# Cached attention and MLP, two passes on one core: paired K transfers, a split last V, an earlier output preparation, a norm in two powers, half blocks on two queues, and another pace for row 0

## The chip, the cores and the metric

The kernel runs on one core of one Trainium2 chip. Its time is the device time in microseconds (us). For the kernel before, five runs gave 1109.03 to 1117.27 us, with a median of 1114.41 us. One further execution was recorded by the hardware profiler. All stage times below come from that execution, counted from the start of its span.

## What is computed

Eight rows of 448 values (B = 8, one token each) go through four residual blocks: attention over a cached K and V, an MLP block, and the same two again with the same weights and the same caches.

```python
def _A_ref(x, k_cache, v_cache, wq, wo):      # 16 query heads, 8 K/V heads, 4096 positions, 256 per head
    q = (x @ wq).reshape(B, Sq, Hq, Dh).transpose(0, 2, 1, 3)
    k = jnp.repeat(k_cache, rep, axis=1); v = jnp.repeat(v_cache, rep, axis=1)
    p = _softmax(jnp.einsum("bhqd,bhkd->bhqk", q, k) * (Dh ** -0.5), axis=-1)
    o = jnp.einsum("bhqk,bhkd->bhqd", p, v)
    return o.transpose(0, 2, 1, 3).reshape(B, Sq, Hq * Dh) @ wo
...
x = A_x
x = x + _A_ref(_layernorm(x, axis=-1), A_k_cache, A_v_cache, A_wq, A_wo)
x = x + _B_ref(_layernorm(x, axis=-1), B_w1, B_w2, B_w3, B_w4)
x = x + _A_ref(_layernorm(x, axis=-1), A_k_cache, A_v_cache, A_wq, A_wo)
x = x + _B_ref(_layernorm(x, axis=-1), B_w1, B_w2, B_w3, B_w4)
```

With one token per row the shifts inside `_B_ref` leave nothing of its first half, so the kernel computes only `x + gelu(layernorm(x) @ w3) @ w4` there, with two layernorms in a row folded into one helper (`norm` with `twice`).

The K cache and the V cache hold 134 MB each in bf16. A row's second pass needs the result of its first pass, so a row's K and V are wanted twice.

## The kernel before

The caches are cut into tiles of 1 MB: 128 partitions of 8 KB. A pair of K/V heads (`gp`, four of them) of one row has four K tiles and four V tiles. A K tile takes, for each partition, one contiguous run of 8 KB out of that partition's 32 KB of the cache, so that two neighbouring K tiles (c = 0 and 1, or 2 and 3) are neighbours in memory as well. Tiles lie in 15 "places", slices of one SBUF tile (`places_t`, `slots`).

The work is a list of 512 items (`items`, L532 to L541), one for each use of a tile, in which the K tiles of one head pair alternate with the V tiles of the pair before. `ps` is the pass (0 or 1), `b` the row, `n` the task, `c` the tile's number. Eleven K and V tiles of each row (`kept`, L63) stay in their places between the first and the second pass, and a twelfth (`inner`) waits in PSUM. That leaves 416 loads instead of 512. While the eleven tiles of a row stay, four places are left for everything that streams by. When the second pass has used them, their places come free within a few items.

`emit_loads` (L603) is called after each item. It takes the loads in order, asks `place_for` (L575) for a free place, and issues one DMA of 1 MB on SP's queue at L624. A load that finds no place ends the call, and those behind it wait as well. For K tiles of the heads that stay, `place_for` looks for two adjacent places and reserves the second (`held`). If two such tiles do lie side by side, `scores` multiplies both in one instruction of 256 columns instead of two of 128 (`also`, L817).

For a K item the VectorE makes two 32x32 block transposes (L632, `transpose_k`) and TensorE the scores (L647). After every second K tile ScalarE makes the exponentials (L656). For a V item TensorE accumulates the product of the probabilities with V (L702). In the last row's last two head pairs the outputs come as columns (`pv_cols`, L716), followed at once by their share of the output projection (`add_cols`, L337). SP's loads wait on semaphores for the place's last reader, and each also waits for the transfer eight before it, since eight DMA semaphores are used in turn.

The small work of a row (the output projection's halves, norms, MLP, next query) is cut into steps of Python generators (`first_half`, `chain`, `first_last`, `last`, `rest`), and `step` (L754) slips one step of each kind in twice per item. `add_gen` takes the items between which a generator is to be spread. Only one generator of a kind runs at a time: the `chain` of row 0 starts when its `first_half` is through.

`load_split` (L160) brings a weight of 448 input rows: three blocks of 128 rows, then the last 64 rows in two halves of columns, one to partitions 0 to 63 (L163) and one to partitions 64 to 127 (L164).

`norm` (L196) forms 1/sqrt as a power on GpSimd (L241). With `twice` it forms two values for each row in one instruction: value 1 scales what goes into the next matmul (`xb`, L261), value 0 updates the residual (L272). For one row or four rows in the MLP this is 2 or 8 values.

After the loop (L885 on) the residual is updated, an fp32 identity (`ident2`) and a zeroed PSUM tile (`o_row`) are made, the last four rows' MLP is run, and the four quarters of the output are written.

Of the kernel before, what the change touches and what calls it, by code (L numbers as in the profile page):

```python
# [8 lines left out]
FP32 = mybir.dt.float32  # L9
# [3 lines left out]
ALU = mybir.AluOpType  # L13
EPS = 1e-5
# [3 lines left out]
def kernel(  # L18
# [27 lines left out]
    nc = tc.nc  # L46
# [14 lines left out]
    NC = 15  # L61
# [98 lines left out]
    def load_split(t, src, cols):  # L160
        for fc in range(3):
            nc.sync.dma_start(t[:, fc * cols : (fc + 1) * cols], src[fc * 128 : fc * 128 + 128, :])
        nc.sync.dma_start(t[0:64, 3 * cols :], src[384:448, 0 : cols // 2])  # L163
        nc.sync.dma_start(t[64:128, 3 * cols :], src[384:448, cols // 2 :])  # L164

    wq_sb = split_tile(HD, "wq_sb")
    w3_sb = split_tile(F, "w3_sb")
# [28 lines left out]
    def norm(x, nb, twice):  # L196

        def room(name, shape, at):  # L200
            n = shape[0] * shape[1]
            if nb < Bn:
                t = chn.tile([128, n * MID], FP32, tag=name)
                ap = t[:, 0 : n * nb]
            else:
                ap = scratch(at, n * nb)
            return ap.rearrange("p (s f b) -> p s f b", s=shape[0], f=shape[1])

        def bc(ap):
            return ap.unsqueeze(1).to_broadcast([128, 4, nb])  # L210

        xx = room("xx", (2, 4), 0)
        nc.vector.tensor_mul(xx[:, 0], x, wv[:].unsqueeze(2).to_broadcast([128, 4, nb]))
        nc.vector.tensor_mul(xx[:, 1], xx[:, 0], x)
        xs = room("xs", (1, 2), 512)[:, 0]
        nc.vector.tensor_reduce(
            xs, xx.rearrange("p s f b -> p s b f"), mybir.AxisListType.X, ALU.add
        )
        yield
        st = room_ps("st", nb).rearrange("p (s b) -> p s b", b=nb)  # L220
        nc.tensor.matmul(st, ones, xs, start=True, stop=True)
        yield
        mv = room("mv", (1, 2), 528)[:, 0]
        nc.vector.tensor_copy(mv, st)
        var = room("var", (1, 1), 608)[:, 0, 0]
        if nb == 1:
            nc.vector.scalar_tensor_tensor(
                var, mv[:, 0], mv[:, 0], mv[:, 1], ALU.mult, ALU.subtract, reverse1=True
            )
        else:  # L230
            nc.vector.tensor_mul(var, mv[:, 0], mv[:, 0])
            nc.vector.tensor_sub(var, mv[:, 1], var)


        ve = room("ve", (1, 2), 544)[:, 0]
        n = 2 if twice else 1
        nc.vector.tensor_scalar(ve[:, 0], var, 0.0, EPS, ALU.max, ALU.add)
        if twice:
            nc.vector.tensor_scalar(ve[:, 1], var, 0.0, EPS * EPS / (1 + EPS), ALU.max, ALU.add)
        rs = room("rs", (1, 2), 560)[:, 0]  # L240
        nc.gpsimd.tensor_tensor(  # L241
            rs[:, 0:n].rearrange("p n b -> p (n b)"),
            ve[:, 0:n].rearrange("p n b -> p (n b)"),
            nhalf[:].to_broadcast([128, n * nb]),
            ALU.pow,
        )
        xc = room("xc", (1, 4), 576)[:, 0]
        nc.vector.tensor_tensor(xc, x, bc(mv[:, 0]), ALU.subtract)  # L248
        yield
        if nb > 1:  # L250
            yield
        c = (1 + EPS) ** -0.5 if twice else 1.0
        rl = rs[:, n - 1]
        parts = ((0, 128, 0, 0, 3, 0), (0, 64, 64, 3, 4, 3), (64, 128, 64, 3, 4, 4))
        for p0, p1, x0, f0, f1, to in parts:
            pp = slice(x0, x0 + p1 - p0)
            dst = xbs(nb)[p0:p1, to : to + f1 - f0, :]
            if nb == 1:
                nc.vector.tensor_scalar(dst, xc[pp, f0:f1], rl[pp], c, ALU.mult, ALU.mult)
            else:  # L260
                nc.vector.scalar_tensor_tensor(  # L261
                    dst,
                    xc[pp, f0:f1],
                    c,
                    rl[pp].unsqueeze(1).to_broadcast([p1 - p0, f1 - f0, nb]),
                    ALU.mult,
                    ALU.mult,
                )
        if twice and nb == 1:
            nc.vector.scalar_tensor_tensor(x, xc, rs[:, 0], x, ALU.mult, ALU.add)  # L270
        elif twice:
            nc.vector.tensor_tensor(xc, xc, bc(rs[:, 0]), ALU.mult)  # L272
            nc.vector.tensor_add(x, x, xc)
        yield
# [175 lines left out]
    def first_half(b, st):  # L450

        OT = work.tile([128, 2, Hq, 1], BF16, tag="OT", bufs=1)
        st["OT"] = OT
        yield from half(st["o", 0], st["z"], 0, OT[:, :, :, 0])
        yield from add_cols(
            y_room(1)[:, 0], lambda i: OT[:, i % 2, i // 2], wo_sb, range(NB2 // 2), 1
        )
# [85 lines left out]
    def stays(it):  # L543
        n, kv, c = it
        return (tasks[n][2], kv, c) in kept
# [10 lines left out]

    held = {}
    AHEAD = 4

    def paired(n, c):  # L560

        ps, _, gp = tasks[n]
        u = c - c % 2
        if ps == 0:
            return gp in keep
        return all((gp, 0, k) in kept for k in (u, u + 1))
# [8 lines left out]
    def place_for(it):  # L575

        n, kv, c = it
        if it in held:
            p = held.pop(it)
            if p not in places:  # L580
                held[it] = p
                return None
            places.remove(p)
        else:
            open_ = [p for p in places if p not in held.values()]
            if not open_:
                return None
            p = open_[0]
            if kv == 0 and c % 2 == 0 and paired(n, c):
                two = [  # L590
                    (max(free_at[q], now[0]), k, p1, q)
                    for k, p1 in enumerate(open_)
                    for q in (p1 + 1, p1 - 1)
                    if 0 <= q < NC and q not in held.values() and free_at[q] <= now[0] + AHEAD
                ]
                if two:
                    _, _, p, q = min(two)
                    held[n, 0, c + 1] = q
            places.remove(p)
        free_at[p] = again[tasks[n][1:], kv, c] if tasks[n][0] == 0 and stays(it) else used_at[it]  # L600
        return p

    def emit_loads(most=None):  # L603
        n = 0
        while loads and places and n != most:
            it = loads[0]
            p = place_for(it)
            if p is None:
                break
            del loads[0]  # L610
            where[it] = p
            if stays(it):
                where[tasks[it[0]][1:], it[1:]] = p
            t, kv, c = it
            _, b, gp = tasks[t]
            dst = slots[p]
            rows = (A_v_cache if kv else A_k_cache)[b, 2 * gp : 2 * gp + 2].rearrange(
                "g s d -> (g s) d"
            )
            if kv:  # L620
                src = rows.rearrange("(a p y) d -> a p (y d)", a=4, y=16)[c]
            else:
                src = rows.rearrange("(p x y) d -> x p (y d)", x=4, y=16)[c]
            nc.sync.dma_start(dst[:], src)  # L624
            n += 1

    def transpose_k(t):
# [123 lines left out]
    def add_gen(kind, b, g, at, until, total):  # L751
        gens.append({"kind": kind, "b": b, "g": g, "at": at, "until": until, "n": 0, "of": total})
# [20 lines left out]
    rz_gp = None  # L773

    for idx, it in enumerate(items):
        n, kv, c = it
        ps, b, gp = tasks[n]
        if (ps, b, gp, kv, c) == (0, Bn - 1, REST, 0, 0):
# [50 lines left out]
        else:  # L829
# [34 lines left out]
            if c == 3:  # L864
                done = pairs_done[ps, b] = pairs_done.get((ps, b), 0) + 1
                if done == 2 and ps == 0:
                    add_gen("chain", b, first_half(b, st), idx + 1, idx + 21, 10)
                elif done == 2:
                    add_gen("chain" if final else "last", b, first_last(b, st), idx + 1, idx + 13, 9)
                elif done == 4 and ps == 0:  # L870
                    add_gen("chain", b, chain(b, st), idx + 1, first_of[(1, b), 0] - 1, 38)
                elif done == 4 and not final:
                    add_gen("last", b, last(b, st), idx + 1, idx + (7 if b == Bn - 2 else 13), 6)
# [8 lines left out]
        step(10 * len(items))  # L882


    end = [slots[p] for p in places[:2]]  # L885
    xs = xT[:, :, MID:]
    nc.vector.tensor_add(xs, xs, st["y"])
    ident2 = end[0][:, 0:256].bitcast(FP32)
    nc.vector.tensor_copy(ident2, identb[:])
    W = D // 4  # L890
    o_row = store[0][:, 0:W]
    nc.vector.memset(o_row, 0.0)
    run(mlp_hidden(MID, Bn - MID))
    for q in range(4):
        for fc in range(4):
# [57 lines left out]
```

The softmax here doesn't subtract the row's maximum and nothing guards it: scores larger than these inputs give would overflow.

## Time and profile before

| what | us |
|---|---|
| median of five runs | 1114.41 |
| the profiled execution: its time | 1115.8 |
| the profiled execution: its span | 1114.0 |
| TensorE busy in matmuls / in weight loads | 663.6 / 461.3 |
| VectorE busy | 592.9 |
| ScalarE busy | 124.3 |
| GpSimd busy | 15.7 |
| VectorE idle until a K tile landed | 278.3 |
| TensorE idle until a V tile landed | 89.4 |
| last matmuls on the last V tile start | 1099.93 |

Busy time is the sum of the instructions of an engine[...]. 448.96 MB pass over the DMA engines in the span, a mean of 403 GB/s. The granted TensorE clock was full until about 190 us and then mostly half, 0.636 in the mean.

### The profile page before, as it was taken

The page shows a single profiled execution, that of the slowest core. Times are in us where ns is not written, and L with a number is a line of the kernel's source. Part 1 is how long each engine was busy: PE and PEld are TensorE (multiplying, and loading weights), DVE is VectorE, ACT ScalarE, POOL GpSimd, SP SyncE. Part 2 cuts the span into 40 slices and gives each one's busy share as a digit, 9 for nine tenths or more (in the row PEclk, how much of TensorE's full clock was granted, in tenths as well). Part 3 has the DMA queues.
Part 4 walks back from the last instruction along what each step waited for, and adds up shares of the span by engine and source line. Part 5 has one row for each costly group of instructions (what it writes and reads, how often), then busy time and mean ns, then how long its engine had stood idle before and what let it go on. Part 6 is the DMA issues. An engine that isn't in the chain of part 4 may idle for free. (4 is left out here: it accounts for less than half of the span.)

```text
span 1114.0 us, 33816 instructions
## 1 busy us (share of the span) xinstructions
PE 663.6 (60%) x15606; PEld 461.3 (41%) x15606; DVE 592.9 (53%) x1010; ACT 124.3 (11%) x362; POOL 15.7 (1%) x25
## 2 busy tenths in 40 slices
PE   3135568546863577446774467834676467757764
PEld 2123345334542355224552245623454244535554
DVE  5155554746365555556465553655628453675462
ACT  0001001110110011100020001100111101111110
POOL 0000000000000000000000000000000000000000
PEclk9999999655565556665575555655557555665575
DMA  9999999999999999999999999999999999999993
GB/s 356 386 421 420 415 377 409 419 419 391 414 419 420 390 415 420 418 420 402 410 420 420 420 406 408 419 420 412 393 399 420 413 396 406 419 419 398 410 418 164
DMA packets 65181, 448.96 MB, mean 403 GB/s; under 512 B 6920, under 2 KB 10896, under 8 KB 11408
## 3 DMA queue, kind: packets, MB, share of 16 engines
q1 hardware_dynamic: 65008, 446.80, 98.2%
q8 instruction: 122, 2.00, 0.7%
q14 instruction: 19, 0.16, 0.0%
q10 hardware_dynamic: 32, 0.00, 0.0%
HBM read 446.77 MB, written 0.01 MB: 401 GB/s over the span
## 5 line engine op out<-in xcount | busy, mean ns | idle before, releaser
L632 DVE STREAM_TRANSPOSE places<-places 128x1024 uint32<-128x1024 uint32 x400 | 469.5, 1219 | 280.8 <-DMA places<-in_A_k_cache_dram 278.3
L647 PE MATMUL sc<-places,qbd 128*8 128x128 bf16 (+1 forms) x7072 | 268.0, 304 | 296.8 <-DVE places L632 252.3
L647 PEld LDWEIGHTS <-qbd 128*8 128x8 bf16 x7072 | 168.6, 105 | 371.3 <-issue 183.6
L702 PE MATMUL o<-places,ptw 128*8 128x256 bf16 x3968 | 243.9, 389 | 104.4 <-DMA places<-in_A_v_cache_dram 89.4
L656 ACT ACTIVATE p_n<-sc 128x256 bf16<-128x256 f32 x128 | 95.5, 746 | 834.7 <-PE sc L647 834.7
L702 PEld LDWEIGHTS <-ptw 128*8 128x8 bf16 x3968 | 114.1, 110 | 150.4 <-issue 109.5
L337 PEld LDWEIGHTS <-wo_sb 128*128 128x128 bf16 x1280 | 38.6, 102 | 21.9 <-issue 21.6
L284 PEld LDWEIGHTS <-wq_sb 128*128 128x128 bf16 x1152 | 35.7, 104 | 25.8 <-issue 19.0
L310 DVE TENSOR_SCALAR qbd<-misc,quad 128x64 bf16<-128x64 f32 x64 | 13.8, 278 | 53.9 <-PE misc L304 53.9
L284 PE MATMUL misc<-xb,wq_sb 128*128 128x1 bf16 x1024 | 34.5, 165 | 4.8 <-ACT ptw L690 2.8
L337 PE MATMUL misc<-OT,wo_sb 128*128 128x1 bf16 x1024 | 34.8, 165 | 2.0 <-issue 2.0
L656 ACT ACTIVATION_READ_ACCUMULATOR p_n<-sc 128x1 f32 x128 | 33.5, 262 | 0.0
L441 PEld LDWEIGHTS misc<-R,o_sb 128*128 128x128 f32 x124 | 27.9, 311 | 10.6 <-issue 9.8
L690 ACT CAST ptw<-misc 128x128 bf16<-128x128 f32 x64 | 17.5, 274 | 120.8 <-PE misc L683 65.1
L441 PE MATMUL misc<-R,o_sb 128*128 128x8 f32 x124 | 30.5, 357 | 0.2
L241 POOL TENSOR_TENSOR t<-t,nhalf 128x2 f32<-128x2 f32 (+2 forms) x18 | 13.3, 741 | 1084.4 <-DVE t L248 1084.4
L674 DVE STREAM_TRANSPOSE places<-store 128x512 uint32<-128x512 uint32 x32 | 20.1, 685 | 11.5 <-PE sc L647 11.5
L410 PE MATMUL misc<-zm,one 128*128 128x8 f32 (+1 forms) x66 | 19.1, 362 | 4.3 <-ACT ptw L690 2.4
L355 PEld LDWEIGHTS <-w_sb 128*128 128x128 bf16 x560 | 17.2, 105 | 10.4 <-issue 9.2
L355 PE MATMUL misc<-xb,w_sb 128*128 128x1 bf16 (+1 forms) x560 | 18.6, 166 | 4.1 <-DVE xb L261 2.9
L410 PEld LDWEIGHTS misc<-zm,one 128*128 128x128 f32 x66 | 16.2, 304 | 11.0 <-issue 3.7
L445 DVE CAST OT<-misc 128x16 bf16<-128x16 f32 x16 | 2.4, 153 | 34.0 <-PE misc L441 31.3
(93 smaller groups left out, 245.6 us busy)
## 6 DMA issues: line engine op xcount, KB each, us to landing
places<-in_A_v_cache_dram SPq DMA_DIRECT2D x216, 1024.0 KB, 10.7
places<-in_A_k_cache_dram SPq DMA_DIRECT2D x200, 1024.0 KB, 11.9
wo_sb<-in_A_wo_dram SPq DMA_DIRECT2D x1, 3584.0 KB, 25.6
wq_sb<-in_A_wq_dram SPq DMA_DIRECT2D x3, 1024.0 KB, 7.0
w_sb<-in_B_w_dram SPq DMA_DIRECT2D x1, 1568.0 KB, 15.2
w_sb<-in_B_w_dram SPq DMA_DIRECT2D x3, 448.0 KB, 25.6
wq_sb<-in_A_wq_dram SPq DMA_DIRECT2D x2, 256.0 KB, 10.1
w_sb<-in_B_w_dram SPq DMA_DIRECT2D x2, 112.0 KB
```

The source lines that it names most:

```text
L284: nc.tensor.matmul(q_ps[:, j * Hq + h, :], w, xbs(nb)[:, xi, :], start=(fc == 0), stop=(fc == 3),)
L310: nc.vector.tensor_scalar_mul(qbd[:, :, :, a, :], qs.rearrange("p e (f g u h) -> p (e f) u g h", f=2, u=2, h=2)[:, :, u], quad[:, a : a + 1],)
L337: nc.tensor.matmul(y_ps[:, fc, :], w[:, i, at : at + 128], rhs(i), start=start, stop=stop, skip_group_check=open is not None,)
L355: nc.tensor.matmul(h_ps[:, c * nb : c * nb + nb], w, xbs(nb)[:, xi, :], start=(fc == 0), stop=(fc == 3),)
L410: nc.tensor.matmul(z_ps, ones, zm[:], start=True, stop=True)
L441: nc.tensor.matmul(ot_ps[:, j], o_sb[:].rearrange("p (i j) -> p j i", j=2)[:, j], R[:], start=True, stop=True)
L632: nc.vector.transpose(w, w)
L647: nc.tensor.matmul(sc[32 * k : 32 * k + 8, 128 * x : 128 * (x + nx)], qbd[:, ep, gp].rearrange("p a h -> p (a h)"), v, start=(n == 0), sto ...
L656: nc.scalar.activation(p_sb[:, :, :, 2 * u : 2 * u + 2].rearrange("p t i x -> p x t i"), sc[:, 256 * u : 256 * u + 256].rearrange("p (x t ...
L674: nc.vector.transpose(slot[:].bitcast(U32)[:, 512 * n : 512 * n + 512], store[n][:].bitcast(U32))
L690: nc.scalar.copy(ptw[:, :, :, 6:8], pt_ps.rearrange("p t k (a h) -> p a (t k) h", a=4),)
L702: nc.tensor.matmul(o_ps[32 * q : 32 * q + 8, 0:256], ptz[:, at : at + 8], v[:, y * Dh : (y + 1) * Dh], start=(begin and y < 4), stop=(y >= ...
```

## The change

- `both_for` is new. For an even K tile of a head pair that stays, in the first pass, it looks for two adjacent places that are free or will be within four items, if at least seven loaded tiles are still to be used and the mate is among the next three loads. `emit_loads` then issues both tiles as one DMA of 2 MB with runs of 16 KB, ahead of the V tile that stood between them. If the two places are not free yet, it stops there, and the loads behind it wait.
- The very last load is issued as two DMAs of 512 KB, each of all 128 partitions and half of the columns.
- `ident2` and `o_row` are made two items before the end of the loop.
- `norm` with `twice` and more than one row makes two powers: first that of value 1, then that of value 0.
- The second half block of a weight is issued on ScalarE's queue.
- The `first_half` of row 0 is spread over 15 items instead of 20.

```diff
@@ load_split
-        nc.sync.dma_start(t[64:128, 3 * cols :], src[384:448, cols // 2 :])
+        nc.scalar.dma_start(t[64:128, 3 * cols :], src[384:448, cols // 2 :])
@@ norm
-        nc.vector.tensor_scalar(ve[:, 0], var, 0.0, EPS, ALU.max, ALU.add)
+        rs = room("rs", (1, 2), 560)[:, 0]
+
+        def power(k0, k1):
+            nc.gpsimd.tensor_tensor(
+                rs[:, k0:k1].rearrange("p n b -> p (n b)"),
+                ve[:, k0:k1].rearrange("p n b -> p (n b)"),
+                nhalf[:].to_broadcast([128, (k1 - k0) * nb]),
+                ALU.pow,
+            )
+
         if twice:
             nc.vector.tensor_scalar(ve[:, 1], var, 0.0, EPS * EPS / (1 + EPS), ALU.max, ALU.add)
-        rs = room("rs", (1, 2), 560)[:, 0]
-        nc.gpsimd.tensor_tensor(
...
-        )
+            if nb > 1:
+                power(1, 2)
+        nc.vector.tensor_scalar(ve[:, 0], var, 0.0, EPS, ALU.max, ALU.add)
+        power(0, 2 if twice and nb == 1 else 1)
@@ planner
+    QUEUED = 7
...
+    def both_for(it):
+
+        n, kv, c = it
+        mate = (n, 0, c + 1)
+        if it not in held:
+            if kv or c % 2 or tasks[n][0] or not paired(n, c) or mate not in loads[:3]:
+                return None
+            open_ = [p for p in range(NC) if p in places or free_at[p] >= 0]
+            two = [
+                (max(free_at[q] if q not in places else -1 for q in (p, p + 1)), p)
+                for p in open_
+                if p + 1 in open_ and not {p, p + 1} & set(held.values())
+            ]
+            two = [t for t in two if t[0] <= now[0] + AHEAD]
+            if not two or sum(used_at[i] > now[0] for i in where if i in used_at) < QUEUED:
+                return None
+            p = min(two)[1]
+            held[it], held[mate] = p, p + 1
+        if held.get(mate) != held[it] + 1:
+            return None
+        return held[it], mate
@@ emit_loads
+            both = both_for(it)
+            if both:
+                p, mate = both
+                if p not in places or p + 1 not in places:
+                    break
+                for i, q in ((it, p), (mate, p + 1)):
+                    loads.remove(i)
+                    places.remove(q)
+                    del held[i]
+                    taken(i, q)
+                _, b, gp = tasks[it[0]]
+                nc.sync.dma_start(
+                    places_t[:, p * PB : (p + 2) * PB],
+                    A_k_cache[b, 2 * gp : 2 * gp + 2]
+                    .rearrange("g s d -> (g s) d")
+                    .rearrange("(p u z) d -> u p (z d)", u=2, z=32)[it[2] // 2],
+                )
+                n += 1
+                continue
...
-            nc.sync.dma_start(dst[:], src)
+            if loads:
+                nc.sync.dma_start(dst[:], src)
+            else:
+                for y in range(2):
+                    nc.sync.dma_start(
+                        dst[:, 8 * Dh * y : 8 * Dh * (y + 1)], src[:, 8 * Dh * y : 8 * Dh * (y + 1)]
+                    )
@@ the loop over the items
+        if idx == len(items) - 2:
+            end = [slots[p] for p in places[:2]]
+            ident2 = end[0][:, 0:256].bitcast(FP32)
+            nc.vector.tensor_copy(ident2, identb[:])
+            W = D // 4
+            o_row = store[0][:, 0:W]
+            nc.vector.memset(o_row, 0.0)
...
-                    add_gen("chain", b, first_half(b, st), idx + 1, idx + 21, 10)
+                    add_gen("chain", b, first_half(b, st), idx + 1, idx + (16 if b == 0 else 21), 10)
@@ after the loop
-    end = [slots[p] for p in places[:2]]
     xs = xT[:, :, MID:]
     nc.vector.tensor_add(xs, xs, st["y"])
-    ident2 = end[0][:, 0:256].bitcast(FP32)
-    nc.vector.tensor_copy(ident2, identb[:])
-    W = D // 4
-    o_row = store[0][:, 0:W]
-    nc.vector.memset(o_row, 0.0)
```

More of the change, by code (lines that the diff above doesn't have):

```diff
@@ L236, in norm @@
         n = 2 if twice else 1
-        nc.vector.tensor_scalar(ve[:, 0], var, 0.0, EPS, ALU.max, ALU.add)
+        rs = room("rs", (1, 2), 560)[:, 0]
[6 more added lines that the diff above has]
+            )
         if twice:
             nc.vector.tensor_scalar(ve[:, 1], var, 0.0, EPS * EPS / (1 + EPS), ALU.max, ALU.add)
-        rs = room("rs", (1, 2), 560)[:, 0]
[L241 to L245, printed above, removed]
-        )
+            if nb > 1:
+                power(1, 2)
+        nc.vector.tensor_scalar(ve[:, 0], var, 0.0, EPS, ALU.max, ALU.add)
+        power(0, 2 if twice and nb == 1 else 1)
         xc = room("xc", (1, 4), 576)[:, 0]
@@ L599, in place_for, with taken @@
             places.remove(p)
+        return p
+    def both_for(it):
[18 more added lines that the diff above has]
+        return held[it], mate
+    def taken(it, p):
+        where[it] = p
+        n, kv, c = it
+        if stays(it):
+            where[tasks[n][1:], it[1:]] = p
         free_at[p] = again[tasks[n][1:], kv, c] if tasks[n][0] == 0 and stays(it) else used_at[it]
-        return p
     def emit_loads(most=None):
@@ L610, in emit_loads @@
             del loads[0]
-            where[it] = p
-            if stays(it):
-                where[tasks[it[0]][1:], it[1:]] = p
+            taken(it, p)
             t, kv, c = it
```

## The prediction

> **What bounds the kernel now.** I read the page's busy shares and slices first, then the waits by engine, then SP's queue in order of time, then DMA rates in chosen stretches, and last the timeline from the final load to the end.
>
> ```profile
> PE 663.6 (60%) x15606; PEld 461.3 (41%) x15606; DVE 592.9 (53%) x1010; ACT 124.3 (11%) x362; POOL 15.7 (1%) x25
> DMA  9999999999999999999999999999999999999993
> GB/s 356 386 421 420 415 377 409 419 419 391 414 419 420 390 415 420 418 420 402 410 420 420 420 406 408 419 420 412 393 399 420 413 396 406 419 419 398 410 418 164
> q1 hardware_dynamic: 65008, 446.80, 98.2%
> ```
>
> No engine is busy for more than 60%, while the DMA engines are at 9 tenths in every slice but the last. 420 GB/s comes back again and again, and nothing exceeds it by more than 1: the transfers are the bound. At 421 GB/s the 446.8 MB of SP's queue would take 1061 us. They end with the last V tile at 1099.9 us, so some 37 us are lost in the slices below 415, and 14 us follow the last landing.
>
> ```profile
> DVE places L632 <- DMA places<-in_A_k_cache_dram: 278.3, 130, 21.1
> PE o L702 <- DMA places<-in_A_v_cache_dram: 89.4, 39, 17.9
> ```
>
> The engines wait for the tiles, not the tiles for the engines, over most of the span. SP's queue shows two regimes:
>
> ```profile
> 66.40 0.33 SPq L624 DMA_DIRECT2D places<-in_A_k_cache_dram  x1
> 68.89 0.33 SPq L624 DMA_DIRECT2D places<-in_A_v_cache_dram  x1
> 71.36 0.33 SPq L624 DMA_DIRECT2D places<-in_A_k_cache_dram  x1
> ...
> 249.39 0.33 SPq L624 DMA_DIRECT2D places<-in_A_k_cache_dram  x1
> 251.29 0.33 SPq L624 DMA_DIRECT2D places<-in_A_v_cache_dram  x1
> 254.35 0.33 SPq L624 DMA_DIRECT2D places<-in_A_k_cache_dram  x1
> 256.14 0.33 SPq L624 DMA_DIRECT2D places<-in_A_v_cache_dram  x1
> ```
>
> At 66 to 71 us one tile is issued every 2.48 us, and the landing comes 19.8 us after the issue, which is eight tiles of 2.48 us: the queue is full and the limit is the transfer itself. At 250 us, where eleven places are held for the second pass, landing takes 7 to 9 us and issues come unevenly, as the four remaining places come free. The rate there sinks to 390 GB/s (250 to 275 us). The 37 lost us lie mostly in such stretches and in the small-run weights before 50 us.
>
> ```profile
> 28.00:36.00 8.00, 2.01 (x52) 1.34 (x52) 2.40 (x3) 1.01 (x3) 0.00 (x0) 1.00 1.06 386
> 66.00:100.00 34.00, 13.94 (x216) 7.55 (x216) 19.58 (x22) 2.75 (x8) 0.00 (x0) 1.00 1.01 421
> ...
> 10.20:13.50 3.30, 0.19 (x1) 0.10 (x1) 0.00 (x0) 0.00 (x0) 0.00 (x0) 1.00 1.01 287
> ```
>
> The last two columns are the DMA share and GB/s: `wo` in runs of 1792 B moves at 386, tiles in runs of 8 KB at 421, the half blocks of `wq` at 287.
>
> [...]16 engines at 386 GB/s take 74.3 ns for a run of 1792 B, at 421 GB/s 311.3 ns for 8192 B; the line through both has 7.9 ns fixed. [...]
>
> **The change, part by part.** The sum is made against the profiled execution's 1115.8 us (span 1114.0), which is 1.4 us above the median of 1114.41.
>
> *Pairs.* Counted in the order of the changed program, 23 of the 416 loads become pairs (4 in row 0, 2 in row 1, 4, 4, 3, 4, 1, 1), and SP issues 23 DMAs fewer. Each pair spares one run of every two: 128 runs, 8 on each engine, 8 x 7.9 = 63 ns. 23 x 0.063 = 1.5 us. All of it counts, as the pairs lie in full-queue stretches where the computing follows the landings: the exponentials start some 3 us after their K tile lands (two transposes of 1.2 us and 0.6 us of matmuls). Bounds: 0, if long runs are cut up again, and about 3, twice the line's intercept.
>
> The price could be delay. A pair's first tile lands 2.48 us later, and so does the V tile it overtakes; the second K tile is no later. Its transposes (2 x 1.2) then run while the overtaken V lands, so the second K tile's scores and the second V end where they did. I take 0. The pair also waits for the later of two places, with up to four free places unused behind it on SP's queue. For row 5, the longest wait, I lined it up with the trace: the pair waits for item 313, done at 702.7 us, when the transfers in flight reach to 708.2. The next waits for item 316, about 707, with work to 718. So the DMA engines do not run dry; without that lead each would cost up to 2.5 us.
>
> Adjacent places also become more frequent: 256 score instructions of 256 columns replace 512 of 128. That spares TensorE some 4 us (32 of 256 columns took 1.88 us, four times 16 of 128 columns 2.4), where it is not the limit: 0.
>
> *Half blocks.* From 10.2 to 13.5 us 287 instead of 421 GB/s cost 3.3 x (1 - 287/421) = 1.05 us. With the second half beside the full-width blocks, [...]only the first half still runs alone. The halves of `w3` are less than half as large. I take 0.8, bounds 0 and 1.2. ScalarE issues two DMAs at its start; its first exponential is at 24.35 us, so that is hidden. SP's next DMAs come 0.6 us earlier into a full queue: nothing.
>
> *Row 0.* The chain of row 0 starts at item 36 instead of 38. Its norm moves from items 43 and 44, where row 2's query is spread (TensorE L304 at 147.40, VectorE L310 at 147.87), to 40 and 41. In the trace that meeting holds back one issue for 5.1 us (146.83 to 151.94), and a landing comes 2 us late. Part of that comes back elsewhere, since two steps for each item are still the limit. I take 0.8, bounds -1 and 2.5.
>
> *The end.* The timeline from the last landing:
>
> ```profile
> 1099.93 1.02 PE L716 MATMUL store<-ptw,places 128*128 128x2 bf16 x32 [1.44 <-DMA places<-in_A_v_cache_dram]
> ...
> 1101.84 0.17 DVE L887 TENSOR_TENSOR xT<-xT,store 128x16 f32<-128x16 f32 x1 [0.63 <-PE store L337]
> 1101.93 0.22 DVE L889 CAST places<-identb 128x128 f32<-128x128 bf16 x1
> 1102.17 0.15 DVE L892 MEMSET store<- 128x112 f32 x1
> ...
> 1104.52 1.65 POOL L241 TENSOR_TENSOR t<-t,nhalf 128x8 f32<-128x8 f32 x1 [70.14 <-DVE t L248]
> 1106.19 0.55 DVE L261 SCALAR_TENSOR_TENSOR xb<-t 128x12 bf16<-128x12 f32 x3 [1.75 <-POOL t L241]
> ```
>
> Split V: half of the 32 matmuls run before the last half lands, 0.51 us; the second DMA adds 8 runs per engine at 7.9 ns, 0.06. Gain 0.45. Tiles ahead: L889 and L892 leave the path, 0.3 us (L213 follows L887 directly); they then lie in VectorE's long waits between the last V tiles. Their own wait is for the DMA that last wrote that place, long landed. Norm in halves: a power of 8 values takes 1.65 us, of 2 values 0.70, of 1 value 0.55, so about 0.158 per value and 1.02 for 4. It also starts one VectorE instruction earlier, 0.1. Gain 0.75[...]. The second power ends about 1 us after the first, and L272 waits for it behind L261 on VectorE; behind L272 only L373 is queued, which needs the 1.74 us of matmuls L355 anyway. Next late is then L355. Together 1.5, bounds 1.0 and 1.7.
>
> Sum: 1.5 + 0.8 + 0.8 + 1.5 = 4.6 us. 1115.8 becomes 1111.2, and the median 1114.4 becomes 1109.8.
>
> **The rivals.**
> - *Long runs bring nothing and row 0 gives nothing*: the engines cut 16 KB up again. What speaks for it: no run this long of the tiles is in the trace. 4.6 - 1.5 - 0.8 = 2.3 spared: 1112.1.
> - *More than the sum*: pairs hold fewer of the eight semaphores, SP wakes less often, and the earlier landings carry into the four-place stretches. If a fifth of the 30 us lost there goes, 1109.8 - 6 = 1103.8. For it: those stretches are the largest loss. Against it: in them no pair is issued at all.
> - *Slower: the pair's late first tile.* Where the computing is already at the landings (14 of the 23, in row 0 and the last head pair of rows), the VectorE gets four transposes, 4.8 us, in a row, and small work behind them in its queue (query spread 0.86 us, norm steps) is late, so that places come free late at the start of the four-place stretch. At 1 us each that is 14, less 4.6: 1123.8. It decides from 0.33 us for each of the 14; the eight transfers in flight (19.8 us) speak against it.
>
> **How the numbers follow.** The sum 0.68, nothing from long runs 0.10, more 0.10, slower 0.12. A measurement of this kernel can tell about 0.5%, 5.6 us, from no change. The likeliest case's own range is 1105 to 1114; its centre is inside the band, 1.0 us from its edge at 1108.8, so 0.46 of it counts as faster (0.31) and 0.54 as the same (0.37). The second case is the same, the third faster, and of the last 0.09 is slower and 0.03 the same: faster 0.41, same 0.50, slower 0.09. The bounds of the parts give 1114.4 - 8.4 and 1114.4 - 0; for eight in ten I add some spread of the runs and part of the rivals: 1104 to 1115.5.
>
> **What would show it.** Right: in full-queue stretches a pair takes about 4.9 us where two tiles took 4.97; 10 to 13.5 us runs above 350 GB/s; from the last V matmuls to the end about 1.5 us less; the dips of the GB/s row stay where they are, in the four-place stretches. Wrong: new dips where the pairs are issued, a K wait at L632 well above 278 us, or L272 between L261 and a late L373. The forecast falls if the landing interval in full-queue stretches changes by more than 1%, as then 16 KB runs cost or spare more than 8 runs' fixed time.

## The result and the profile after

| | us |
|---|---|
| before, median (78 runs) | 1114.1 |
| changed, median (41 runs) | 1112.9 |
| ratio, with its 95% interval | 0.9984 [0.9972, 0.9996] |
| that is | 1.8 less (0.4 to 3.1) |
| changed, the profiled execution: time / span | 1108.93 / 1107.1 |
| last V matmuls to the end of the span, before / changed | 14.1 / 12.9 |

The changed kernel is faster, but by less than 0.5%. That is the case which the forecast held likeliest; the time is 3.1 us above the forecast one. The interval excludes both no change and the forecast gain of 4.6 us. The profiled execution of the changed kernel is one of its shorter ones (its 41 runs reach from 1103.19 to 1118.9, and it is the eighth). The 6.9 us between the two profiled executions are therefore not the gain, and the sizes below are read from single stretches and from repeated runs.

The page of the changed kernel: busy times, the DMA share and rate in 40 slices, the row of SP's queue (packets, MB, share of the engines' time), and two rows of the DMA issues (count, KB each, us from issue to landing).

```profile
PE 668.5 (60%) x15350; PEld 460.7 (42%) x15350; DVE 590.6 (53%) x1010; ACT 124.2 (11%) x362; POOL 16.4 (1%) x27
...
DMA  9999999999999999999999999999999999999994
GB/s 347 387 424 422 417 401 419 420 411 412 421 421 421 401 419 421 425 418 405 419 423 420 419 398 415 420 422 408 404 410 421 414 387 400 422 416 369 410 420 191
...
q1 hardware_dynamic: 61680, 446.42, 98.2%
...
places<-in_A_k_cache_dram SPq DMA_DIRECT2D x23, 2048.0 KB, 16.2
...
places<-in_A_v_cache_dram SPq DMA_DIRECT2D x2, 512.0 KB, 18.3
```

The bound is the same: no engine is busy for more than 60%, and the DMA engines are full in every slice but the last. There are 23 pairs and 2 half V tiles. TensorE has 256 matmuls fewer, the pairs' score instructions of 256 columns. The dips of the rate lie where the four-place stretches are, as before. The first slice lost 9 GB/s (356 before); this is where the half blocks are.

The waits by engine of the changed kernel (us in total, times, longest); L691 and L761 are the former L632 and L702:

```profile
DVE places L691 <- DMA places<-in_A_k_cache_dram: 269.2, 116, 20.4
...
PE o L761 <- DMA places<-in_A_v_cache_dram: 123.7, 38, 17.3
```

TensorE waits 34 us more for V. This belongs to the pairs: the wait is 84 to 92 us in the traces of before, e1_halves, e1_row0 and e1_end, which have no pairs and K tiles in runs of 8 KB, and 120 to 132 us in all the traces with pairs. A pair pushes the V tile that it overtakes some 2.4 us back (an estimate: the pair's 4.905 us of the queue instead of a single tile's 2.485, both read below). The 9 us less at VectorE are not clear of the spread (273 to 284 us without pairs, 269 to 278 with them). These are waits for tiles of a queue that is full; their sum says nothing of the end, which came earlier.

SP's queue of the changed kernel in order of time, in a full stretch (time, us, line; L654 issues a pair, L678 a single tile):

```profile
54.23 0.33 SPq L654 DMA_DIRECT2D places<-in_A_k_cache_dram  x1
56.71 2.81 SPq L678 DMA_DIRECT2D places<-in_A_v_cache_dram  x2
61.67 0.33 SPq L654 DMA_DIRECT2D places<-in_A_k_cache_dram  x1
64.14 5.24 SPq L678 DMA_DIRECT2D places<-in_A_v_cache_dram  x2
71.55 0.33 SPq L654 DMA_DIRECT2D places<-in_A_k_cache_dram  x1
74.01 5.23 SPq L678 DMA_DIRECT2D places<-in_A_v_cache_dram  x2
```

Each issue waits for the transfer eight before, so the gaps show what those transfers took: 2.48 us behind a single tile and about 4.9 us behind a pair (the two V issues within the row of 64.14 lie 4.91 us apart). The landings give the number more finely: in full stretches the median from one landing to the next is 2.485 us for single tiles (trace of before) and 4.905 us for the few pairs whose landing the trace tells (4.90 to 4.92 in four traces with pairs). That is 0.065 us spared per pair, and 23 x 0.065 = 1.5 us.

The timeline of the changed kernel from the last landing (start, us of the group, engine, line, and in brackets what was waited for):

```profile
1092.96 0.51 PEld L775 LDWEIGHTS <-places 128*128 128x128 bf16 x16 [0.30 <-DMA places<-in_A_v_cache_dram]
...
1094.21 0.59 PE L775 MATMUL store<-ptw,places 128*128 128x2 bf16 x16 [0.66 <-DMA places<-in_A_v_cache_dram]
...
1095.71 0.17 DVE L952 TENSOR_TENSOR xT<-xT,store 128x16 f32<-128x16 f32 x1 [0.63 <-PE store L343]
1095.91 0.17 DVE L213 TENSOR_TENSOR t<-xT,wv 128x16 f32<-128x16 f32 x1
...
1098.14 2.00 POOL L240 TENSOR_TENSOR t<-t,nhalf 128x4 f32<-128x4 f32 x2 [68.74 <-DVE t L254]
1099.19 0.55 DVE L267 SCALAR_TENSOR_TENSOR xb<-t 128x12 bf16<-128x12 f32 x3 [1.05 <-POOL t L240]
1099.42 1.75 PE L361 MATMUL misc<-xb,w_sb 128*128 128x4 bf16 x56 [2.23 <-DVE xb L267]
1100.17 0.18 DVE L278 TENSOR_TENSOR t<-t 128x16 f32<-128x16 f32 x1 [0.42 <-POOL t L240]
...
1101.20 0.22 DVE L379 TENSOR_SCALAR g_t<-misc 128x56 f32<-128x56 f32 x1 [0.65 <-PE misc L361]
```

Sixteen matmuls instead of 32 follow the last landing (L775, the former L716). L213 follows L952 directly, where two instructions stood between. VectorE waits 1.05 us for the power instead of 1.75. L278, which needs the second power, ends at 1100.35, while L379 behind it waits for the matmuls of L361 until 1101.20: the second power is hidden.

### The profile page after: what moved, and what is told of

It reads as the page before. It is cut to its first block, busy times and chain, and to the rows that moved or that the text cites. A ratio compares the mean times of both kernels' runs of the same rounds, so it can differ in the third digit from the quotient of the medians.

```text
span 1107.1 us, 33251 instructions
## 1 busy us (share of the span) xinstructions
PE 668.5 (60%) x15350; PEld 460.7 (42%) x15350; DVE 590.6 (53%) x1010; ACT 124.2 (11%) x362; POOL 16.4 (1%) x27
## 5 line engine op out<-in xcount | busy, mean ns | idle before, releaser
L691 DVE STREAM_TRANSPOSE places<-places 128x1024 uint32<-128x1024 uint32 x400 | 468.2, 1218 | 276.0 <-DMA places<-in_A_k_cache_dram 269.2
L706 PE MATMUL sc<-places,qbd 128*8 128x128 bf16 (+1 forms) x6816 | 271.0, 313 | 252.7 <-DVE places L691 203.1
L761 PE MATMUL o<-places,ptw 128*8 128x256 bf16 x3968 | 246.2, 393 | 135.5 <-DMA places<-in_A_v_cache_dram 123.7
L761 PEld LDWEIGHTS <-ptw 128*8 128x8 bf16 x3968 | 114.6, 112 | 183.0 <-issue 141.1
L316 DVE TENSOR_SCALAR qbd<-misc,quad 128x64 bf16<-128x64 f32 x64 | 13.8, 278 | 59.1 <-PE misc L310 59.1
L416 PEld LDWEIGHTS misc<-zm,one 128*128 128x128 f32 x66 | 16.4, 307 | 16.7 <-issue 9.3
L361 PEld LDWEIGHTS <-w_sb 128*128 128x128 bf16 x560 | 17.3, 105 | 10.3 <-issue 10.1
L361 PE MATMUL misc<-xb,w_sb 128*128 128x1 bf16 (+1 forms) x560 | 18.6, 166 | 4.2 <-DVE xb L267 2.2
L726 DVE STREAM_TRANSPOSE store<-places 128x512 uint32<-128x512 uint32 x32 | 20.0, 693 | 1.4 <-DMA places<-in_A_v_cache_dram 1.4
## 6 DMA issues: line engine op xcount, KB each, us to landing
wq_sb<-in_A_wq_dram SPq DMA_DIRECT2D x3, 1024.0 KB, 10.2
```

Source lines behind the costliest of these rows:

```text
L361: nc.tensor.matmul(h_ps[:, c * nb : c * nb + nb], w, xbs(nb)[:, xi, :], start=(fc == 0), stop=(fc == 3),)
L416: nc.tensor.matmul(z_ps, ones, zm[:], start=True, stop=True)
L691: nc.vector.transpose(w, w)
L706: nc.tensor.matmul(sc[32 * k : 32 * k + 8, 128 * x : 128 * (x + nx)], qbd[:, ep, gp].rearrange("p a h -> p (a h)"), v, start=(n == 0), sto ...
L726: nc.vector.transpose(store[n][:].bitcast(U32), slot[:].bitcast(U32)[:, 512 * n : 512 * n + 512])
L761: nc.tensor.matmul(o_ps[32 * q : 32 * q + 8, 0:256], ptz[:, at : at + 8], v[:, y * Dh : (y + 1) * Dh], start=(begin and y < 4), stop=(y >= ...
```

## The experiments

The theory (A) is that of the prediction: fixed time per run of bytes, half blocks side by side, less meeting of norm and query in row 0, a shorter end. The rival (B) is that the change's gain is only the end, with the pairs either worth nothing or given back by late tiles. The experiments were run in three groups (e1, e2, e3), each with the kernel before beside it, whose medians were 1114.43, 1115.66 and 1115.84 us. A difference below is the median of before times (ratio - 1), with the interval of the ratio. Differences of the bare medians deviate from it by up to 1.5 us (e1_halves: +0.1), so only the intervals should be leant on.

| kernel | median us | ratio, 95% | difference us |
|---|---|---|---|
| e1_halves | 1114.56 | 1.0014 [0.9997, 1.0030] | +1.6 (-0.3 to +3.3) |
| e1_pairs | 1111.64 | 0.9977 [0.9958, 0.9995] | -2.6 (-4.7 to -0.6) |
| e1_row0 | 1113.10 | 0.9991 [0.9967, 1.0016] | -1.0 (-3.7 to +1.8) |
| e1_end | 1113.45 | 0.9995 [0.9975, 1.0015] | -0.6 (-2.8 to +1.7) |
| e2_no_halves | 1111.14 | 0.9966 [0.9947, 0.9984] | -3.8 (-5.9 to -1.8) |
| e2_halves_first | 1111.64 | 0.9968 [0.9947, 0.9990] | -3.6 (-5.9 to -1.1) |
| e2_queued0 | 1115.74 | 1.0004 [0.9984, 1.0025] | +0.4 (-1.8 to +2.8) |
| e3_after | 1111.38 | 0.9962 [0.9942, 0.9982] | -4.2 (-6.5 to -2.0) |
| e3_no_halves | 1109.50 | 0.9953 [0.9932, 0.9974] | -5.2 (-7.6 to -2.9) |
| e3_pairs_end | 1113.21 | 0.9971 [0.9952, 0.9991] | -3.2 (-5.4 to -1.0) |

e2_short_runs was run once: 1185.46 us.

### Each part alone

**e1_pairs**: the kernel before with only `both_for` and the joined DMA.

```diff
+            both = both_for(it)
...
+                nc.sync.dma_start(
+                    places_t[:, p * PB : (p + 2) * PB],
```

> Only the K pairs in one transfer. Theory A: a pair takes 4.90 to 4.92 us of the full queue instead of 4.97, 23 x 0.07 = 1.6 us saved, and all of it reaches the end. Theory B: the queue saves it, but the four-place stretches take it back, 0 us. Theory C (late first tiles): slower by 2 us or more, with more VectorE wait for K tiles.

2.6 us less, and the interval excludes zero. The size agrees with the 1.5 us from the landings. That pairs bring nothing, or are given back by a late first tile, does not fit this kernel's runs.

The rival that the engines cut 16 KB up again is settled by the packets of SP's queue (before 65008), here in the page of e1_pairs:

```profile
q1 hardware_dynamic: 61696, 446.80, 98.4%
```

That is 3312 packets less, or 144 for each of the 23 pairs: the 128 runs that are joined, and 16 more. The trace lists 2944 = 23 x 128 packets of 16 KB on this queue, so a run of 16 KB stays one packet. The other 16 are packets of 4 bytes, which come with every DMA. Spread over the 16 engines, a pair spares 9 packets on each and not 8, and the 65 ns are some 7 ns for each packet.

**e1_halves**: the kernel before with one word changed.

```diff
-        nc.sync.dma_start(t[64:128, 3 * cols :], src[384:448, cols // 2 :])
+        nc.scalar.dma_start(t[64:128, 3 * cols :], src[384:448, cols // 2 :])
```

> Only the second half blocks go to ScalarE's queue. Theory A (the prediction's): 287 GB/s at 10 to 13.5 us is cured, 0.8 us saved; the first K tile is there 0.5 to 1 us earlier once the moved w3 half is allowed for. Theory B (the trace of the changed kernel): the stretch from 3.6 to 10 us loses as much as the later one wins, the first K tile lands about 1.0 us later (17.0 instead of 16.0) and V0 of row 0 at about 49.2 instead of 48.95; the time is the same within 1 us of before, rather 0.2 above than below.

Not faster: 1.6 us more, with an interval that just includes zero. The forecast 0.8 us of gain lies outside it. The section on the half blocks shows why the gain is missing.

**e1_row0**: the kernel before with only the other pace.

```diff
-                    add_gen("chain", b, first_half(b, st), idx + 1, idx + 21, 10)
+                    add_gen("chain", b, first_half(b, st), idx + 1, idx + (16 if b == 0 else 21), 10)
```

> Only the pace of row 0's first half. Theory A: fewer late landings between 140 and 178 us, 0.8 to 2.2 us saved. Theory B: the landings of that stretch move within what any two runs differ by, 0 us (between -0.7 and +0.7).

The interval holds both 0 and the forecast. The trace tells of the mechanism (below): the hold is still there.

**e1_end**: the kernel before with only the split last V tile, the two tiles made ahead and the norm in two powers.

```diff
+            if loads:
+                nc.sync.dma_start(dst[:], src)
+            else:
+                for y in range(2):
...
+        if idx == len(items) - 2:
...
+            if nb > 1:
+                power(1, 2)
```

> Only the end: split last V, tiles made ahead, norm in two powers. From the last landing to the end of the span 12.9 us instead of 14.1. Theory A: 1.2 us saved in all. Theory B: part of it is lost again because two powers or the two last DMAs cost more in other places: 0.6 us or less.

The runs can't tell 1.5 us from nothing here. The trace can: the last V matmuls start at 1104.17 us and the span ends at 1117.1, 12.9 us as in the changed kernel, against 14.1 before. The same trace shows why single parts are hard to measure: its loads are issued in the order of before. By bytes moved, it is within 0.3 us of before up to 164 us, 1.5 us ahead at 189 us and 4.2 us behind at the last tile. Most of this arises in the four-place stretches, without any change to them.

### The half blocks

Two more kernels. **e2_no_halves** is the changed kernel with the half block back on SP's queue (the line of e1_halves reversed). **e2_halves_first** issues the first half block ahead of the three full blocks, so that both halves start together:

```diff
+        nc.sync.dma_start(t[0:64, 3 * cols :], src[384:448, 0 : cols // 2])
...
-        nc.sync.dma_start(t[0:64, 3 * cols :], src[384:448, 0 : cols // 2])
         nc.scalar.dma_start(t[64:128, 3 * cols :], src[384:448, cols // 2 :])
```

> The whole change, but with the second half blocks back on SP's queue. Theory A (pairs 1.5 us and the end 1.2 us are what the change brings, the half blocks nothing or a loss): 2.7 us or more below before, ratio 0.9976 or lower, first K tile at 16.0 to 16.3 us. Theory B (the half blocks help): not below the whole change, 1.8 us or less under before.

> The whole change, with SP's half block issued ahead of the three full blocks, so that both halves are under way at once. Theory A[...]: the rate from 3.6 to 20 us rises from 376 GB/s to about 410, the first K tile lands at about 16 us with 112 KB more behind it, 0.8 us saved against the whole change. Theory B[...]: about 380 GB/s as before, first K tile at 16.5 us or later.

The windows of the first 20 us; the last column is GB/s. The kernel before:

```profile
3.60:10.00 6.40, 0.80 (x4) 0.70 (x4) 2.67 (x21) 0.66 (x1) 1.64 (x1) 1.00 1.00 422
...
3.60:20.00 16.40, 4.88 (x146) 4.65 (x147) 4.84 (x27) 0.66 (x1) 1.64 (x1) 1.00 1.01 394
```

The changed kernel:

```profile
3.60:10.00 6.40, 0.77 (x3) 0.60 (x3) 2.68 (x21) 0.66 (x1) 1.64 (x1) 1.00 1.01 357
10.20:13.50 3.30, 0.19 (x1) 0.11 (x1) 0.00 (x0) 0.00 (x0) 0.00 (x0) 1.00 1.05 357
3.60:20.00 16.40, 5.04 (x146) 4.57 (x146) 3.96 (x27) 0.66 (x1) 1.64 (x1) 1.00 1.02 376
```

e2_halves_first:

```profile
3.60:10.00 6.40, 0.80 (x3) 0.60 (x3) 2.68 (x21) 0.66 (x1) 1.64 (x1) 1.00 1.01 341
10.20:13.50 3.30, 0.19 (x1) 0.10 (x1) 0.00 (x0) 0.00 (x0) 0.00 (x0) 1.00 1.04 432
3.60:20.00 16.40, 4.97 (x146) 4.62 (x147) 4.58 (x27) 0.66 (x1) 1.64 (x1) 1.00 1.02 393
```

From 10.2 to 13.5 us the rate did rise, from 287 to 357. But from 3.6 to 10 us, where full blocks alone ran at 422, it sank to 357. Over the whole stretch to 20 us it is 376 instead of 394 GB/s. Other traces show how firm this is: 378 in e1_halves, 373 in e2_queued0 and 383 in e3_after, against 386 to 397 in the traces with the half block on SP's queue and K tiles in runs of 8 KB or more. With both halves in flight from the start it is 341 in the first window, 432 in the later one, and 393 over the whole: no loss, and no gain (e2_halves_first's theory A wanted about 410, theory B about 380). Wherever the halves are put, no time is won over the whole stretch. What holds the half blocks back, no trace here shows.

The first K tile lands at 16.0 us before, at 17.0 in the changed kernel, 17.7 in e1_halves and 16.4 in e2_halves_first; some 0.27 us of it are the second halves of `w3`, which now come ahead of it (an estimate: 112 KB at 421 GB/s). By the first V tile, once all weights are in, no loss is to be seen: 48.95 us before, 48.9 to 49.2 with the half blocks on two queues. e2_no_halves came out as its theory A said: 3.8 us less than before, with the first K tile at 16.0 us. Still, the measured cost of the two queues is a hint and not more: +1.6 us alone, and 5.2 against 4.2 us spared without and with them in group e3. Against it stands e2_halves_first, which keeps the two queues and is level with e2_no_halves (3.6 and 3.8 us spared). Where a cost would arise was not found.

### The row-0 pace

**e3_no_halves** repeats the changed kernel with the half block on SP; **e3_pairs_end** has in addition the old pace of row 0; **e3_after** is the changed kernel once more, to have all three beside each other.

```diff
-                    add_gen("chain", b, first_half(b, st), idx + 1, idx + (16 if b == 0 else 21), 10)
+                    add_gen("chain", b, first_half(b, st), idx + 1, idx + 21, 10)
```

> The whole change without the half blocks, a second time. Pairs, row 0 and the end alone: 2.7 to 3.8 us below before if the first measurement holds, ratio 0.9966 to 0.9976.

> As the last, and with row 0's pace as before: pairs and the end alone. Theory A (row 0's pace brings something): 0.8 us or more slower than the last. Theory B (the hold at item 44 is the query spread and its transposes, not the norm, so the pace changes nothing): level with it, 2.7 us below before, and the issues at 147 and 152 us are 4.5 to 5.2 us apart in both.

> The whole change once more, beside the two below on one chip. If the half blocks on ScalarE's queue do nothing it is level with the next one (within 1 us); if they cost what the runs so far hint at, 1.5 to 2 us slower than the next one.

SP's queue around the hold of row 0, in the changed kernel:

```profile
147.16 0.33 SPq L678 DMA_DIRECT2D places<-in_A_v_cache_dram  x1
151.86 0.33 SPq L678 DMA_DIRECT2D places<-in_A_k_cache_dram  x1
```

and in e3_pairs_end, with the old pace:

```profile
146.60 0.33 SPq L678 DMA_DIRECT2D places<-in_A_v_cache_dram  x1
151.70 0.33 SPq L678 DMA_DIRECT2D places<-in_A_k_cache_dram  x1
```

4.7 us against 5.1: the hold did not go (4.7 in e1_row0 and e3_no_halves as well, 5.1 before). The timeline of the changed kernel in that stretch:

```profile
147.56 0.42 PE L310 MATMUL misc<-qT,identb 128*32 128x32 bf16 x16
...
148.03 0.86 DVE L316 TENSOR_SCALAR qbd<-misc,quad 128x64 bf16<-128x64 f32 x4 [2.60 <-PE misc L310]
...
148.81 2.36 DVE L691 STREAM_TRANSPOSE places<-places 128x1024 uint32<-128x1024 uint32 x2
...
151.22 0.60 PE L706 MATMUL sc<-places,qbd 128*8 128x128 bf16 x16 [0.31 <-DVE places L691]
```

No norm is between the two issues any more. What fills them is the spread of row 2's query (L310, L316), the two transposes of the next K tile behind it, and the scores of that tile, which free its place. That tile landed only at 147.23 us (147.24 before). Its transposes and scores, 2.36 and 0.60 us, would by themselves have put the second issue at about 150.3 us (an estimate from these times), so about 3 of the 4.7 us would be there without the query too. The query adds some 1.6 us: VectorE stands idle for 2.60 us, waiting for L310. Moving the norm away took 0.4 us. The runs with the old pace are 2.0 us slower (-3.2 against -5.2), the part alone is 1.0 us faster than before; neither is clear of the intervals. e3_no_halves gained more than the 2.7 to 3.8 us expected of it, and e3_after lies 1.0 us behind it, between its two expectations. That the pace is worth something is possible, but not for the reason given.

### The cost of a run, and the cost of waiting for two places

**e2_short_runs**: the kernel before, with each K tile in four runs of 2 KB for each partition instead of one of 8 KB. The keys then come in another order than V's rows, so it computes another result with equal work.

```diff
-                src = rows.rearrange("(p x y) d -> x p (y d)", x=4, y=16)[c]
+                src = rows.rearrange("(p i x y) d -> x p i (y d)", i=4, x=4, y=4)[c]
+            if not kv:
+                dst = dst.rearrange("p (i w) -> p i w", i=4)
```

> The kernel before, with every K tile in four runs of 2 KB in place of one of 8 KB for each partition, same bytes, still one transfer a tile; the keys of a K tile come in another order than V's rows, so the result is another one at equal work. Theory A (a fixed cost of 7.9 ns for each run): 24 more runs per engine and K tile, 0.19 us each, a K tile takes 2.67 us of the full queue instead of 2.48, 200 x 0.19 = 38 us slower, about 1152 us. Theory B (runs are cut to packets anyway): 0 to 5 us slower.

It took 1185.46 us, 70 us more than before, where theory A expected 38 us. The row of SP's queue, and the window of a full stretch:

```profile
q1 hardware_dynamic: 141808, 446.80, 99.2%
...
66.00:100.00 34.00, 14.35 (x234) 7.82 (x234) 16.97 (x20) 3.77 (x11) 0.00 (x0) 0.73 1.03 404
```

The 76800 packets more than before are 200 K loads x 128 partitions x 3, so each run is one packet. 421 became 404 GB/s, so 1 MB takes 2.595 instead of 2.491 us in the mean. Half of the tiles are K, so a K tile takes about 0.21 us longer for 24 more runs on each engine, or some 9 ns for each: the fixed time of 7.9 ns that the prediction took from weights and tiles holds when a tile's bytes are cut into shorter runs. With 200 loads of K this makes 42 us. The other 28 lie elsewhere; its page shows where:

```profile
GB/s 341 379 405 401 387 344 392 403 384 370 398 403 403 372 375 399 403 404 347 364 403 403 402 350 366 401 404 394 361 372 403 396 344 399 402 400 334 378 401 187
```

Its dips go down to 334 to 372, where before had 377 to 406. Counted by bytes moved, it falls behind by 1.0 us for every 10 MB in full stretches, and by 1.6 to 5 us more in each of the eight four-place stretches, some 26 us in all. Why it loses more there was not shown.

**e2_queued0**: the changed kernel with the condition on the queue's lead removed, which makes 28 pairs instead of 23.

```diff
-    QUEUED = 7
+    QUEUED = 0
```

> The whole change, but pairs are formed however few tiles are queued: 28 pairs instead of 23. Theory A (a pair spares 63 ns and its delay is hidden by the queue): 0.3 us faster than the whole change, not to be told from it. Theory C (the wait for two places costs where the queue is thin): late landings near the new pairs of rows 1, 3, 4, 6 and 7, 2 us or more slower than the whole change.

The gain is gone (1.0004): +0.4 us, where e2_halves_first, which differs otherwise only in the order of the first half block, spared 3.6 in the same group. This is what theory C expected. SP's queue of this kernel around one of the added pairs, in row 0, just after a four-place stretch:

```profile
171.23 0.33 SPq L678 DMA_DIRECT2D places<-in_A_k_cache_dram  x1
...
182.04 0.33 SPq L654 DMA_DIRECT2D places<-in_A_k_cache_dram  x1
```

and the windows there, first of this kernel, then of the changed one:

```profile
170.00:180.00 10.00, 5.96 (x123) 3.86 (x120) 1.30 (x8) 0.00 (x0) 0.00 (x0) 0.50 0.78 323
180.00:190.00 10.00, 8.97 (x163) 5.48 (x164) 5.23 (x9) 2.51 (x7) 0.00 (x0) 0.54 0.70 270
```

```profile
170.00:180.00 10.00, 7.05 (x142) 4.30 (x135) 1.98 (x10) 0.25 (x1) 0.00 (x0) 0.50 1.02 419
180.00:190.00 10.00, 9.46 (x240) 6.50 (x243) 7.16 (x10) 2.26 (x7) 0.00 (x0) 0.68 1.01 421
```

The DMA share is 0.70 instead of 1.01: the engines ran dry while the pair waited for its second place, with 10.8 us between the two issues. The tile ahead landed at 180.34 us and the pair at 190.64; 10.3 us instead of 4.9 leave a hole of 5.4 us. This is the wait for the later of two places, for which the prediction put up to 2.5 us where the lead is missing; the hole is about twice that. It is not the slower rival's mechanism, which was a late first tile with the places free. What keeps the changed kernel from the hole is the lead of at least seven tiles, which a pair may wait through without the queue running dry. In row 5, where the prediction had lined this up, the engines stay full (420 to 421 GB/s from 690 to 720 us in the changed kernel).

## Why the prediction was right, and where it was not

- *The bound and the cover.* Right. The DMA queue stayed the limit, and the added small work and the 23 issues fewer do not show.
- *Pairs, 1.5 us.* Right in mechanism and size: 65 ns per pair measured, 63 forecast; -2.6 us (-4.7 to -0.6) in the runs. The near match has some luck in it, since a pair spares 9 packets on each engine and not 8. The price of 0 for delay holds with a lead of seven tiles: V waits grew by 34 us, and e1_pairs is faster and not slower, against the slower rival. The lead that was lined up for row 5 is the condition: where it is taken away, one pair left a hole of 5.4 us, against the 2.5 us that the prediction allowed for it.
- *Half blocks, 0.8 us.* This is the step that failed. That the second half would cost less beside the full blocks, so that "only the first half still runs alone", was the author's estimate; the trace of before does not have the two side by side. The rate in the narrow window rose as forecast, above 350 GB/s, but the bytes beside it became at least as much slower: 373 to 383 GB/s over the whole stretch, against 386 to 397 with both halves on one queue. No run shows a gain. Whether it is a loss is open: the part alone gives a loss of 1.6 us (-0.3 to +3.3), so that even the lower bound of 0 may have been too high. The prediction's own sign for it, the window from 10 to 13.5 us, could not have shown this, since it held only the place that was relieved.
- *Row 0, 0.8 us.* The mechanism failed: the norm was moved out of the meeting, and the hold of 5.1 us is still 4.7. What held it was the next K tile itself, which landed at 147.23 us, and the query's spread ahead of its transposes. Whether the pace gains something elsewhere (-1.0 and -2.0, neither resolved) is open.
- *The end, 1.5 us.* Right in mechanism, a little too large: 1.2 measured. From the last V matmuls to the next VectorE instruction 0.63 instead of 1.05, so 0.42 (forecast 0.45); the tiles ahead 0.19 (forecast 0.3, since the two instructions, 0.22 and 0.15 us long, cost less in a row than their sum); from the norm's start to `xb` 2.86 instead of 3.55, so 0.69 (forecast 0.75). These three make 1.30. After `xb` the changed kernel takes 0.1 us longer, all of it from the issue of the output DMAs to the end (2.77 against 2.67 us), where nothing was changed. The two powers take 2.00 us, twice 1.0. The matmuls of L361 were next late, as forecast.
- *The sum.* 1.5 + 1.2 are read from the traces. With the half blocks at 0 to -1.6 and row 0 at 0 to +1, this makes 1.1 to 3.7 us. Two comparisons of the changed kernel gave 1.8 and 4.2, weighted by their intervals 2.4. Of the missing 2.8 us in the first, the half blocks' absent gain accounts for 0.8, row 0 for up to 0.8 and the end for 0.3; the rest is within the interval. That the time still fell where it was forecast owes much to the width of the forecast: its range, 1104 to 1115.5 us, holds the kernel before as well (1114.1), and two of the four parts in the sum did not work as described.
- *A version that may be better.* The changed kernel with the half block on SP's queue was 3.8 and 5.2 us faster than before, weighted 4.4. It has the lowest median in both groups. Its lead over the changed kernel in group e3, 1.0 us by the table and 1.9 by the medians, is not resolved, and e2_halves_first is level with it. The 2.7 us read from the traces lie at the edge of what its two intervals allow together (about 2.8 to 6.0), so the rival "more than the sum" is not excluded: earlier landings may carry on into the four-place stretches. No experiment tests it.

## What to carry to other kernels

Joining runs paid even at 8 KB, where the queue of transfers is the bound, but by little: in this kernel the saving was the number of packets spared on one engine times 7 to 9 ns, and it was kept only where the queue had enough in flight to cover the wait for two places (without that lead one pair left a hole of 5.4 us). When a slow transfer is moved beside a fast one, take the rate over the whole stretch that holds both, never over the window that was slow; the relieved window looked better here (357 instead of 287 GB/s) although nothing was won (376 instead of 394 over the whole). Before costing the removal of a stall, list every instruction between the two issues, and look when the data that the second one waits for has landed. The instruction that is moved may have stood only beside the one that holds.

## What was not expected of the hardware

- In these runs the fixed time per packet came out as nearly one number from 1792 B to 16 KB: 7.9 ns (line through two rows of before), about 9 ns (2 KB against 8 KB), 7.2 ns (65 ns for 9 packets, 8 KB against 16 KB). A run of any of these lengths is one packet, and the packets of 4 bytes that come with each DMA take 9 ns in the trace of before (median of 6872).
- In the stretches where few places are free, more runs cost more than their share of time: some 26 of the 70 us of e2_short_runs are lost there beyond what its loads add in full stretches.
- Half blocks of 64 partitions each, both in flight on two queues beside full blocks, ran at 341 GB/s together, less than the full blocks alone at 422; over the whole stretch the rate was 393 against 394.
- A GpSimd power of 4 values took 1.05 us to its consumer, and two in a row 2.00 us, against 1.65 for one of 8 values: the split costs 0.35 us in all, and it pays only because the second is hidden.
